# Which engine subtracts the low parts of queries and keys in an attention and mixer kernel

## The chip, the cores and the metric

The program runs on one core of a Trainium2 chip. The metric is device time in microseconds (us) of one execution, of which three were taken of the kernel before. The engines are TensorE (PE; its weight loads are PEld), VectorE (DVE), ScalarE (ACT) and GpSimd (POOL); SyncE (SP) issues most of the DMAs. Each engine works through its own instruction queue in order, and instructions on different engines are ordered by semaphores.

## The reference

Causal attention with a cumulative decay bias over 4 batches of 8 heads (576 positions, head size 64), then two feed-forward blocks. Cut to what matters here:

```
scores = scale * np.matmul(q, k.transpose(0, 1, 3, 2))
cum = np.cumsum(np.maximum(s, 0.0), axis=-1)
scores = where(causal, -1e9, scores + minimum(-(cum_i - cum_j), 0))
attn = softmax(scores)
attn_out = np.matmul(attn, v)                  # 4 x 8 heads
x = moe(x)        # mix with previous row, relu(xk @ w_k)^2 @ w_v, gate sigmoid(xr @ w_r)
out = u + relu(u @ w_ch1) @ w_ch2              # u = x + token mixing of x
```

## The kernel before

All large products are made in the fp32r format. To keep fp32 precision an operand is split: its high part is the value rounded to fp32r, its low part is the value minus the high part, also in fp32r, and a product is the sum of high*high, high*low and low*high. High parts are written by a ScalarE copy, low parts by a subtraction on VectorE or GpSimd.

The program has three stretches. First come the eight heads of batch 0 in plain fp32 (`early`, `late`). Then 24 heads of batches 1 to 3 (`visits`, with split operands) run as 108 items of one block of 128 query rows each (`attention_item`). A pair of heads shares one item for its last 64 rows each; the transposes of line 445 occur once per pair. In between stand the units of the first feed-forward block (`up`, `gate`, `down`, matrix products on line 107; `mix` on lines 509 to 512 prepares their inputs). The last stretch is the rest of the feed-forward work.

For head i, `place(i)` prepares queries and keys in two tiles. RQ holds the raw values (64 partitions, 2 x 576 columns: y = 0 queries, y = 1 keys). X1 gets the high parts on one half of its partitions (line 255, ScalarE) and the bias rows on the other. X2 gets the high part on one half (a DMA from X1, line 257, issued by SP) and the low part on the other (line 260, the subtraction). One matmul with X1 (line 300) and one with X2 (line 301) then give a block of scores. `place(i + 1)` is called with the first item of head i, thus one head ahead.

An item's chain runs over all engines. `scores`: matmuls into PSUM (3 buffers "s"), the mask and the row maximum on VectorE (line 271, which frees the buffer), then `softmax`: the exponential on ScalarE (282), a small addition on GpSimd (283), a reciprocal on VectorE (284), the scaling of P on GpSimd (285). `transposes`: P is transposed on TensorE (430, 445), its high part copied by ScalarE (439, 448, 452, 458), its low part subtracted on VectorE (440, 449, 453, 459) into PF or PT. `values`: the products with V (488) into one PSUM buffer, which ScalarE (491) and VectorE (494) empty into xt. The values V are split on VectorE (77) and GpSimd (244).

The order on each queue is not written by hand. The code gives each piece a place (`at`), and a scheduler that plays the program through against a model of the engines picks the next instruction by place and by readiness. So when one instruction goes to another engine, the order on all engines behind it can come out anew.

Of the kernel before, what the change touches and what calls it, by code (L numbers as in the profile page):

```python
# [14 lines left out]
ALU = mybir.AluOpType  # L15
# [4 lines left out]
def f32(ap):  # L20
    return ap.bitcast(F32)
# [3 lines left out]
def attention_moe_mixer(  # L25
# [16 lines left out]
    nc = tc.nc  # L42
    G, D, _, S = qk.shape
# [24 lines left out]
    def at(place):  # L68
        return tc.high_priority(tc.cur_priority - int(place * 1000))
# [62 lines left out]
    def x_tile(slot, dtype=F32):  # L132
        return qk_p.tile([128, 2 * S], dtype, tag=f"X{slot}", name=f"X{slot}").rearrange("p (t s) -> p t s", t=2)
# [79 lines left out]
    def xs(i):  # L213
        return X1[i % 2], X2[i % 2]

    def sides(i):
        a, z = slice(0, D), slice(D, 2 * D)
        return (a, z) if i % 2 == 0 else (z, a)

    def raw_qk():  # L220
        if "RQ" not in act:
            act["RQ"] = qk_p.tile([128, 8 * QC], F32, tag="HX", name="RQ")
        return act["RQ"][:, 0:2 * S].rearrange("p (t s) -> p t s", t=2)

    def load(i):
        nc.sync.dma_start(out=raw_qk()[sides(i)[0]], in_=qk[visits[i][0]])
# [19 lines left out]
    def place(i):  # L246
        g = visits[i][0]
        if i < 2:
            X2[i] = x_tile(2 + i, F32R)
        x1, x2 = xs(i)  # L250
        a, z = sides(i)
        rq = raw_qk()[a]
        nc.sync.dma_start(out=f32(x1[z][0:4]), in_=ext_d[g])
        for y in (1, 0):
            nc.scalar.activation(out=x1[a, y], in_=rq[:, y], func=AF.Copy)  # L255
            high, low = (z, a) if y else (a, z)
            nc.sync.dma_start(out=f32(x2[high, y]), in_=f32(x1[a, y]))
            for c in range(2):
                cs = slice(S * c // 2, S * (c + 1) // 2)
                nc.gpsimd.tensor_tensor(out=x2[low, y, cs], in0=rq[:, y, cs], in1=f32(x1[a, y, cs]), op=ALU.subtract)  # L260
        if i + 2 < len(visits):
            load(i + 2)

# [376 lines left out]
    def attention_item(n):  # L640
        if n < N1:
# [22 lines left out]
            if h == H - 1 and j == 2:  # L664
                with at(N0 + n):
                    place(0)
# [8 lines left out]
        if j == 0 and i + 1 < len(visits):  # L675
            with at(N0 + n):
                place(i + 1)
# [98 lines left out]
    for b in range(B):  # L776
        u = moe_units(b)
        x0 = base + PER * (b - 1) + starts[b] if b else 0
        x1 = base + PER * b + ends[b]
        if b == 0:  # L780
            x1 = base + PER + ends[0]
# [5 lines left out]
            x1 = base + 1  # L787
        else:
            x0, x1 = x0 + PER, x1 + PER
# [218 lines left out]
```

## Time and profile before

| | us |
|---|---|
| median of 3 runs | 880.22 (879.58 to 882.47) |
| the profiled execution | 883.16 |
| span of the profiled execution (first to last instruction) | 881.4 |
| TensorE busy | 850.3 (96%) |
| VectorE busy | 491.0 (56%) |
| ScalarE busy | 464.1 (53%) |
| GpSimd busy | 382.1 (43%) |

The profile is one execution. The profiled execution is 2.9 us over the median of the runs, and 1.8 us of it lie outside the span. Busy shares are means over stretches that differ: GpSimd has nothing to do after 600 us, and the subtractions that the change touches lie between 117 and 402 us. Matmuls overlap in their pipeline, so a busy TensorE is not TensorE at its peak.

### The profile page before, as it was taken

The page shows a single profiled execution, that of the slowest core. Times are in us where ns is not written, and L with a number is a line of the kernel's source. Part 1 is how long each engine was busy: PE and PEld are TensorE (multiplying, and loading weights), DVE is VectorE, ACT ScalarE, POOL GpSimd, SP SyncE. Part 2 cuts the span into 40 slices and gives each one's busy share as a digit, 9 for nine tenths or more (in the row PEclk, how much of TensorE's full clock was granted, in tenths as well). Part 3 has the DMA queues.
Part 4 walks back from the last instruction along what each step waited for, and adds up shares of the span by engine and source line. Part 5 has one row for each costly group of instructions (what it writes and reads, how often), then busy time and mean ns, then how long its engine had stood idle before and what let it go on. Part 6 is the DMA issues. An engine that isn't in the chain of part 4 may idle for free. (4 is left out here: it accounts for less than half of the span.)

```text
span 881.4 us, 17425 instructions
## 1 busy us (share of the span) xinstructions
PE 850.3 (96%) x6127; PEld 793.7 (90%) x6127; DVE 491.0 (56%) x1352; ACT 464.1 (53%) x1257; POOL 382.1 (43%) x649
## 2 busy tenths in 40 slices
PE   8889998999999999999999999899999999999998
PEld 5656766888988999989999889899999999999998
DVE  5697765477779575895559865961331222322321
ACT  4688846787785866968567873850320211211210
POOL 4565567688786766866256854630000000000000
PEclk9699999999999999999999999999999999999999
DMA  7953423134322223220144655563021112112100
GB/s 206 249 135 91 120 68 91 28 84 103 87 69 61 67 63 94 61 67 22 31 130 128 203 164 193 181 187 107 16 78 60 44 36 67 42 37 67 44 25 25
DMA packets 64982, 80.02 MB, mean 91 GB/s; under 512 B 9616, under 2 KB 51600, under 8 KB 64896
## 3 DMA queue, kind: packets, MB, share of 16 engines
q1 hardware_dynamic: 58368, 63.24, 26.1%
q0 software_dynamic: 4576, 15.08, 5.5%
q8 instruction: 48, 0.79, 0.4%
q10 hardware_dynamic: 1952, 0.60, 0.3%
q14 instruction: 38, 0.31, 0.1%
HBM read 56.50 MB, written 14.75 MB: 81 GB/s over the span
## 5 line engine op out<-in xcount | busy, mean ns | idle before, releaser
L847 ACT ACTIVATE HID<-c 128x256 fp32r<-128x256 f32 (+1 forms) x96 | 39.3, 409 | 220.4 <-PE c L107 220.3
L107 PE MATMUL vd<-KK,WV 128*128 128x256 f32 (+1 forms) x768 | 120.6, 302 | 0.0
L107 PEld LDWEIGHTS vd<-KK,WV 128*128 128x128 f32 x768 | 107.4, 191 | 4.2 <-issue 2.7
L285 POOL TENSOR_SCALAR P<-P,sum 128x128 f32<-128x128 f32 (+4 forms) x148 | 93.7, 637 | 38.4 <-DVE sum L284 29.1
L107 PE MATMUL h<-XK,WK 128*128 128x320 f32 (+1 forms) x672 | 105.7, 307 | 0.7 <-DVE XK L512 0.6
L107 PE MATMUL c<-HID,WV 128*128 128x256 f32 (+1 forms) x768 | 104.8, 291 | 0.0
L107 PE MATMUL c<-U,WK 128*128 128x256 f32 (+1 forms) x768 | 103.2, 291 | 1.4 <-DVE HID L848 1.4
L282 ACT ACTIVATE P<-P,mx 128x128 f32<-128x128 f32 (+4 forms) x148 | 86.6, 586 | 32.1 <-DVE mx L271 25.4
L107 PEld LDWEIGHTS c<-HID,WV 128*128 128x128 f32 x768 | 100.6, 188 | 0.0
L107 PEld LDWEIGHTS c<-U,WK 128*128 128x128 f32 x768 | 98.6, 188 | 1.7 <-DVE HID L848 1.7
L107 PEld LDWEIGHTS h<-XK,WK 128*128 128x128 f32 x672 | 95.3, 193 | 2.3 <-DVE XK L512 0.8
L271 DVE CUSTOM_DVE_ANT_0 P<-s,maskc 128x128 f32<-128x128 f32 (+4 forms) x148 | 72.0, 498 | 36.9 <-PE t L430 18.2
L848 DVE SCALAR_TENSOR_TENSOR HID<-c,HID 128x256 fp32r<-128x256 f32 (+1 forms) x96 | 43.8, 456 | 81.1 <-ACT HID L847 81.0
L260 POOL TENSOR_TENSOR X<-RQ,X 64x288 fp32r<-64x288 f32 x96 | 78.8, 839 | 13.1 <-ACT X L255 8.0
L912 DVE TENSOR_TENSOR ut<-c,ut 128x256 f32<-128x256 f32 (+1 forms) x32 | 14.6, 458 | 119.3 <-PE c L107 108.3
L524 POOL TENSOR_TENSOR KK<-k,KK 128x256 fp32r<-128x256 f32 (+1 forms) x64 | 54.8, 861 | 17.1 <-ACT k L523 15.5
L107 PE MATMUL r<-XR,WR 128*128 128x320 f32 (+1 forms) x384 | 61.0, 299 | 0.0
L283 POOL TENSOR_SCALAR sum<-sum 128x1 f32<-128x1 f32 (+1 forms) x148 | 33.3, 225 | 54.3 <-ACT P L282 43.0
L107 PE MATMUL c<-HID,WR 128*128 128x256 f32 (+1 forms) x384 | 54.8, 291 | 0.0
L107 PEld LDWEIGHTS r<-XR,WR 128*128 128x128 f32 x384 | 53.0, 188 | 1.2 <-issue 0.9
L107 PE MATMUL c<-U,C1A 128*128 128x256 f32 (+1 forms) x384 | 52.8, 296 | 0.1
L107 PEld LDWEIGHTS c<-U,C1A 128*128 128x128 f32 x384 | 51.5, 190 | 0.3 <-ACT U L897 0.3
(133 smaller groups left out, 1681.3 us busy)
## 6 DMA issues: line engine op xcount, KB each, us to landing
raw<-in_moe_w_ch_dram POOLq DMA_DIRECT2D x48, 256.0 KB, 3.4
RQ<-in_qk_dram SPq DMA_DIRECT2D x24, 288.0 KB
X<-X SPq DMA_DIRECT2D x48, 144.0 KB
yt<-y_d SPq DMA_DIRECT2D x16, 288.0 KB
u_d<-yt SPq DMA_DIRECT2D x16, 288.0 KB
raw<-in_moe_w_k_dram SPq DMA_DIRECT2D x8, 512.0 KB
raw<-in_moe_w_v_dram SPq DMA_DIRECT2D x16, 256.0 KB
ut<-u_d SPq DMA_DIRECT2D x32, 128.0 KB
```

Source lines behind the costliest of these rows:

```text
L107: nc.tensor.matmul(ps, a, b, start=first and i == 0, stop=last and i == n - 1)
L260: nc.gpsimd.tensor_tensor(out=x2[low, y, cs], in0=rq[:, y, cs], in1=f32(x1[a, y, cs]), op=ALU.subtract)
L271: nc.vector.tensor_tensor_reduce(out=P[0:m, c0:c1], in0=ps[0:m, 0:c1 - c0], in1=mask[0:m], scale=-scale, scalar=3.0e38 if x == 0 else mx[0 ...
L282: nc.scalar.activation(out=P[0:m, 0:w], in_=P[0:m, 0:w], func=AF.Exp, bias=mx[0:m, x:x + 1], scale=-1.0, accum_out=sm[0:m, 0:1])
L283: nc.gpsimd.tensor_scalar(out=sm[0:m, 0:1], in0=sm[0:m, 0:1], scalar1=1e-9, scalar2=1.0, op0=ALU.add, op1=ALU.mult)
L285: nc.gpsimd.tensor_scalar(out=P[0:m, 0:w], in0=P[0:m, 0:w], scalar1=sm[0:m, 1:2], scalar2=1.0, op0=ALU.mult, op1=ALU.mult)
L524: nc.gpsimd.tensor_tensor(out=kk[:, 1, m, 0:n], in0=t[:, 0:n], in1=f32(kk[:, 0, m, 0:n]), op=ALU.subtract)
L847: nc.scalar.activation(out=hi, in_=ps, func=AF.Relu)
L848: nc.vector.scalar_tensor_tensor(out=lo, in0=ps, scalar=0.0, in1=f32(hi), op0=ALU.max, op1=ALU.subtract)
L912: nc.vector.tensor_tensor(out=t, in0=ps, in1=t, op=ALU.add)
```

## The change

```diff
             high, low = (z, a) if y else (a, z)
             nc.sync.dma_start(out=f32(x2[high, y]), in_=f32(x1[a, y]))
-            for c in range(2):
-                cs = slice(S * c // 2, S * (c + 1) // 2)
-                nc.gpsimd.tensor_tensor(out=x2[low, y, cs], in0=rq[:, y, cs], in1=f32(x1[a, y, cs]), op=ALU.subtract)
+            nc.vector.tensor_tensor(out=x2[low, y], in0=rq[:, y], in1=f32(x1[a, y]), op=ALU.subtract)
```

Per head GpSimd loses four subtractions of 64 partitions by 288 columns, and VectorE gets two of 64 by 576. The numbers are the same. Lines after 260 move up by two (271 becomes 269, 300 becomes 298).

VectorE's queue where the two heads after the first batch are placed, around 144 to 152 us of the trace: the maxima (the rows ISA) of the third head's blocks stand among the two mixes. Before:

```order
L77 COPY xt<-pv 128x320
L77 CAST VV_1920<-VS 128x2x2x64
L77 CAST VV_1920<-VS 128x3x2x64
L271 ISA P_1889,mx<-s,maskc 128x128
L271 ISA mx 128x1
L509 TENSOR_SCALAR t<-xt,mu 128x320 x2
L440 TENSOR_TENSOR PF<-t,PF 128x384
L271 ISA P_1925,mx<-s,maskc 128x256
L271 ISA mx 128x1
L459 TENSOR_TENSOR PT_1791<-t,PT_1790 128x3x128
L271 ISA P_1949,mx<-s,maskc 128x384
L271 ISA mx 128x1
```

The same place now:

```order
L258 TENSOR_TENSOR X_1561<-RQ,X_1457 64x576 x2
L77 COPY xt<-pv 128x320
L77 CAST VV_1914<-VS 128x2x2x64
L438 TENSOR_TENSOR PF<-t,PF 128x384
L77 CAST VV_1914<-VS 128x3x2x64
L269 ISA P_1919,mx<-s,maskc 128x256
L269 ISA mx 128x1
L269 ISA P_1943,mx<-s,maskc 128x384
L269 ISA mx 128x1
L282 RECIPROCAL sum<-sum 128x1
L507 TENSOR_SCALAR t<-xt,mu 128x320 x2
```

Two subtractions stand ahead of the values' work, and PF and two maxima now stand ahead of the mix where they stood behind its first half.

GpSimd's queue in the same place, where P_1833 (P_1829 now) is the last block of the first pair. Before:

```order
L285 TENSOR_SCALAR P_1794<-P_1794,sum 128x512
L260 TENSOR_TENSOR X_1561<-RQ,X_1457 64x288 x4
L283 TENSOR_SCALAR sum<-sum 128x1
L244 TENSOR_TENSOR VV_1920<-VS,VV_1920 128x2x128
L244 TENSOR_TENSOR VV_1920<-VS,VV_1920 128x3x128
L283 TENSOR_SCALAR sum<-sum 128x1
L260 TENSOR_TENSOR X_1707<-RQ,X_1459 64x288 x4
L283 TENSOR_SCALAR sum<-sum 128x1
L466 MEMSET xt 128x1
L285 TENSOR_SCALAR P_1833<-P_1833,sum 128x576
```

Now:

```order
L283 TENSOR_SCALAR P_1790<-P_1790,sum 128x512
L281 TENSOR_SCALAR sum<-sum 128x1 x2
L244 TENSOR_TENSOR VV_1914<-VS,VV_1914 128x2x128
L244 TENSOR_TENSOR VV_1914<-VS,VV_1914 128x3x128
L283 TENSOR_SCALAR P_1829<-P_1829,sum 128x576
```

The scaling of that block stood behind eight subtractions and stands behind none.

VectorE's queue further on, around 198 us of the trace (P_2577 is that head's fourth block, P_2563 now). Before:

```order
L459 TENSOR_TENSOR PT_1791<-t,PT_1790 128x3x128
L512 TENSOR_TENSOR XK<-t,XK 128x256
L284 RECIPROCAL sum<-sum 128x1
L494 TENSOR_TENSOR xt<-pv,tmp 64x320
L271 ISA P_2577,mx<-s,maskc 128x512
L271 ISA mx 128x1
L459 TENSOR_TENSOR PT_1791<-t,PT_1790 128x4x128
```

Now:

```order
L457 TENSOR_TENSOR PT_1787<-t,PT_1786 128x3x128
L282 RECIPROCAL sum<-sum 128x1
L258 TENSOR_TENSOR X_1705<-RQ,X_1459 64x576
L269 ISA P_2563,mx<-s,maskc 128x512
L269 ISA mx 128x1
L258 TENSOR_TENSOR X_1705<-RQ,X_1459 64x576
L282 RECIPROCAL sum<-sum 128x1
L457 TENSOR_TENSOR PT_1787<-t,PT_1786 128x4x128
```

One subtraction now stands just ahead of a maximum, the other ahead of a reciprocal and of a low part of P.

## Rows read from the trace of the kernel before

**Rows 1.** The page, part 1: busy us (share of the span) and instructions of each engine.

```profile
PE 850.3 (96%) x6127; PEld 793.7 (90%) x6127; DVE 491.0 (56%) x1352; ACT 464.1 (53%) x1257; POOL 382.1 (43%) x649
```

**Rows 2.** Line 260: ns min/median/max; its idle time by releaser; who waited for it.

```profile
L260 POOL TENSOR_TENSOR X<-RQ,X x96: 787/805/1168, 116.9 to 402.2; 64x288 fp32r<-64x288 f32 x96
...
  ACT X L255: 8.0, 5
...
  PEld s L301: 0.6, 1
```

**Rows 3.** Windows: length, busy us (instructions) per engine, clock, DMA; two with half clock.

```profile
110.00:410.00 300.00, 287.62 (x2029) 264.01 (x2028) 214.10 (x659) 216.72 (x576) 220.96 (x387) 0.98 0.28 71
140.00:160.00 20.00, 16.45 (x82) 13.41 (x81) 9.41 (x32) 12.25 (x31) 15.78 (x25) 0.83 0.34 78
260.00:280.00 20.00, 17.56 (x128) 16.48 (x127) 18.85 (x50) 11.58 (x31) 13.41 (x27) 0.91 0.24 62
```

**Rows 4.** Waits of TensorE's weight loads, 110 to 410 us: total us, times, longest.

```profile
PEld s L300 <- DVE mx L271: 6.5, 12, 1.8
PEld pv L488 <- DVE xt L494: 2.8, 4, 1.1
PEld t L430 <- POOL P L285: 2.6, 3, 1.5
...
PEld pv L488 <- DVE PT L449: 1.9, 3, 0.8
PEld pv L488 <- DVE PF L440: 1.7, 1, 1.7
```

**Rows 5.** Windows between line 445's transposes, one a pair; columns as in rows 3.

```profile
182.50:201.40 18.90, 18.10 (x128) 16.73 (x126) 14.22 (x48) 14.24 (x37) 15.12 (x29) 1.00 0.36 93
201.40:220.20 18.80, 18.18 (x128) 16.68 (x126) 13.35 (x49) 13.96 (x36) 15.52 (x30) 1.00 0.35 91
220.20:240.80 20.60, 19.73 (x148) 18.68 (x149) 16.51 (x52) 15.73 (x43) 14.73 (x29) 1.00 0.37 93
240.80:272.20 31.40, 28.20 (x207) 26.29 (x206) 26.18 (x70) 21.93 (x62) 25.75 (x42) 0.95 0.24 60
272.20:293.00 20.80, 20.80 (x166) 20.32 (x166) 16.93 (x57) 14.82 (x39) 14.61 (x29) 1.00 0.33 86
...
346.40:371.70 25.30, 25.30 (x208) 24.58 (x206) 20.55 (x62) 24.19 (x69) 22.03 (x37) 1.00 0.30 75
371.70:398.40 26.70, 24.89 (x199) 23.97 (x197) 25.08 (x70) 15.79 (x43) 18.10 (x32) 1.00 0.24 64
```

**Rows 6.** VectorE and GpSimd groups, 110 to 410 us: busy us, mean ns | idle before.

```profile
L260 POOL TENSOR_TENSOR X<-RQ,X 64x288 fp32r<-64x288 f32 x96 | 78.8, 839 | 13.1 <-ACT X L255 8.0 <-PE s L386 2.3
...
L459 DVE TENSOR_TENSOR PT<-t,PT 128x512 fp32r<-128x512 f32 x21 | 14.3, 682 | 1.3 <-ACT PT L458 1.2
L459 DVE TENSOR_TENSOR PT<-t,PT 128x384 fp32r<-128x384 f32 x22 | 12.0, 544 | 2.1 <-ACT PT L458 2.0
L512 DVE TENSOR_TENSOR XR<-t,XR 128x320 fp32r<-128x320 f32 x12 | 8.6, 731 | 0.0
```

**Rows 7.** Timeline, one mix under GpSimd's subtractions: start us, duration us, instruction [idle before].

```profile
263.26 2.01 POOL L260 TENSOR_TENSOR X<-RQ,X 64x288 fp32r<-64x288 f32 x2
263.29 0.47 DVE L512 TENSOR_TENSOR XK<-t,XK 128x320 fp32r<-128x320 f32 x1
264.54 1.08 DVE L512 TENSOR_TENSOR XK<-t,XK 128x320 fp32r<-128x320 f32 x1
...
265.37 0.86 POOL L285 TENSOR_SCALAR P<-P,sum 128x576 f32<-128x576 f32 x1
...
266.29 0.66 PE L430 MATMUL t<-ident,P 128*128 128x128 f32 x4 [1.25 <-POOL P L285]
```

**Rows 8.** Line 510, 110 to 410 us: ns min/median/max, first and last start, forms.

```profile
L510 DVE SCALAR_TENSOR_TENSOR t<-xt,omu,t x36: 459/640/1079, 126.4 to 392.8; 128x320 f32<-128x320 f32 x20, 128x256 f32<-128x256 f32 x16
```

## The prediction

> **What bounds the kernel now.** I read the shares of the page first. TensorE is busy for 96% of the span, no other engine for more than 56% [rows 1], so in the mean TensorE is the bound, and another engine costs time only where TensorE waits for it. The subtractions in question all start between 117 and 402 us [rows 2], so I look at 110 to 410 us alone. There TensorE is busy for 287.6 of 300 us, VectorE for 214.1 and GpSimd for 221.0 [rows 3]: 12.4 us of idle TensorE are all that a better flow could win back, beside the time under half clock. The clock's mean was 0.83 in 140 to 160 us and 0.91 in 260 to 280 us [rows 3], so 20 x 0.17 = 3.4 us and 20 x 0.09 = 1.8 us of TensorE's full-speed time are missing there; both follow upon waits of TensorE.
>
> For whom does TensorE wait? The waits of its weight loads in this stretch [rows 4]: 6.5 us for the row maximum on VectorE, 2.8 us for the adding of xt, 1.9 and 1.7 us for the low parts of P, 12.9 us of VectorE together. For GpSimd it is 2.6 us (the scaled P) and 0.6 us (the subtraction itself [rows 2]), 3.2 us together. Four fifths of these waits are for the engine that is to get more work.
>
> The windows between the transposes of line 445 show the same by pair of heads [rows 5]. VectorE's share is 75%, 71% and 80% in the three pairs from 182.5 to 240.8 us, 83% in 240.8 to 272.2 us, 81% in 272.2 to 293.0 and in 346.4 to 371.7 us, and 94% in 371.7 to 398.4 us. TensorE idles for 0.8, 0.6, 0.9, 3.2, 0.0, 0.0 and 1.8 us in these seven. GpSimd is between 68% and 87% in them.
>
> **What goes.** 96 subtractions of 0.839 us, 78.8 us of GpSimd [rows 6]. GpSimd falls from 221.0 to 142 of 300 us, from 74% to 47%. Nearly nobody waited for these results as such (0.6 us, once); they cost as a queue in front of the softmax's scaling. The best place to see that is 263.26 us: two subtractions hold GpSimd for 2.01 us, the scaling of P runs behind them at 265.37 us, and the transposes at 266.29 us come after 1.25 us of idle TensorE [rows 7]. I credit the change with all of GpSimd's waits, -3.2 us.
>
> There is a second credit. Under those two subtractions one subtraction of the mix (line 512, both inputs in SBUF) took 1.08 us, while a like one that began with them took 0.47 us [rows 7]; the mean of the wide shape in the stretch is 0.731 us [rows 6]. So GpSimd's work stretches VectorE's by about 0.26 us an instruction. The stretch holds 36 calls of the mix, by its line 510 [rows 8], of three such instructions each (509, 510, 512). If all 108 are stretched alike, and line 260's share of that is its share of GpSimd's time (79/221 = 0.36), VectorE gets back 108 x 0.26 x 0.36 = 10 us.
>
> **What comes.** 48 subtractions of 64 x 576 on VectorE. The trace has none of that length. Line 459 takes 0.544 us for 384 columns and 0.682 us for 512 [rows 6], 1.08 ns a column, so 576 columns take 0.682 + 64 x 0.00108 = 0.75 us. That is the lower bound, 36 us in all. The new instruction has both inputs in SBUF, as line 512 has, so it is open to the same stretch, at GpSimd's lower share: 0.26 x 47/74 = 0.17 us, giving 0.92 us, 44 us in all. The upper bound adds the whole difference seen once, 1.08 - 0.47 = 0.61 us, to each: 1.36 us, 65 us. I take 44 us, since GpSimd's share is what the 0.731 us is a mean over. Net of the credit VectorE gets 44 - 10 = 34 us (26 to 55), and goes from 214 to 248 of 300 us, from 71% to 83%. The Trainium skill, SBUF — State Buffer, section "Who interferes with whom", has a sharper rule that speaks against this change: a VectorE instruction with two SBUF inputs and a GpSimd instruction that reads SBUF exclude each other for a whole instruction, and the later one waits. By that rule the new subtractions also hold up GpSimd's scalings of P, which the sum here leaves out; the 1.08 us of [rows 7] agrees with it in one direction, and no row here shows the other.
>
> A new wait: the subtraction waits for ScalarE's high part. GpSimd idled 8.0 us in five such waits [rows 2]. On VectorE the same wait would hold maxima and reciprocals behind it. VectorE's new queue puts the instruction where the scheduler expects the high part to be done, so I count one wait of the five, 8.0/5 = 1.6 us; the bounds are none and all 8 us. SP's load of the head after next now waits for VectorE's reading of RQ instead of GpSimd's; it is issued a head ahead, with half of a pair's 18.8 us or more [rows 5] as cover. The matmuls, their DMAs and ScalarE's work stay the same in number.
>
> **What that costs TensorE.** A pair gets four subtractions, 4 x 0.92 = 3.7 us, less about a twelfth of the 10 us (twice that in the two pairs with most of the mix, from 240.8 and from 371.7 us): +2.8 us, or +2.0 us. The shares become 17.0 of 18.9 us (90%), 16.2 of 18.8 (86%), 19.3 of 20.6 (94%), 28.2 of 31.4 (90%), 19.7 of 20.8 (95%), 23.4 of 25.3 (92%), and 27.1 of 26.7 us, over the pair's length. The trace has one pair with VectorE at 94%, where TensorE idles 1.8 of 26.7 us, 6.8% [rows 5]. I let the four pairs that reach 90% or more with little idle time now idle as much: 1.3, 1.4, 1.4 and 1.7 us instead of 0.8, 0.9, 0.0 and 0.0, +4.1 us. The pair from 240.8 us idles 3.2 us already, and I add nothing. The last must get longer to stay at 94%: 27.1/0.94 = 28.8 us, +2.1 us. By the places in the queue this is where it should show: around 198 us a subtraction now stands right ahead of a maximum, and another ahead of a low part of P, both things that TensorE waits for.
>
> **The sum.** +4.1 + 2.1 + 1.6 - 3.2 = +4.6 us on the profiled 883.16 us, 887.8 us; on the median of the runs, 2.9 us lower, 884.8 us, which is the forecast.
>
> **Rival one, faster: GpSimd was the queue that mattered.** TensorE's own waits name the last engine of a chain, and a chain goes through GpSimd twice (lines 283 and 285) but also three times through VectorE. If GpSimd at 74 to 87% made each item late, and VectorE's room in 110 to 410 us (86 us idle) takes the 34 us without new waits, the credit stands alone: -3.2 us of waits, and -1.8 us since the half clock after 266 us follows the wait for P: 875.2 us. If also the first jam goes, another -3.4 us: 871.8 us. For it: at that jam PF and two maxima now stand ahead of the mix, and the scaling of the first pair's last block no longer stands behind eight subtractions. Against it: VectorE gets four of its new subtractions in the same few microseconds, 3.7 us of work. It decides for faster if VectorE stays under some 85% in the pairs that were at 80%. The Trainium skill, GPSIMD Engine Reference, section "4.1 Engine selection", also says to put two-input elementwise work on VectorE, as GpSimd takes about twice as long; here it is 4 x 0.839 against 2 x 0.75 us a head, which agrees, but the rule counts engine time and TensorE is the bound.
>
> **Rival two, no change.** TensorE has matrix products of the feed-forward block to run in any gap, and the whole order from 117 us on comes out anew. If these products fill what VectorE leaves, gains and losses cancel: within 2.6 us of 880.2 us. For it: three of the seven pairs with much VectorE work idle under 0.7 us now [rows 5].
>
> **A worse case of the forecast.** If pairs at 90% idle as the one from 240.8 us does (3.2 of 31.4 us, 10%), the four idle 8.7 instead of 1.7 us, +7.0 us; with the last pair's 2.1 us, two waits for ScalarE, 3.2 us, and no credit, it is +12.3 us: 892.5 us.
>
> **How the numbers follow.** Forecast (VectorE becomes the bound in the dense pairs) 0.47, rival one 0.28, rival two 0.25. A difference of 0.3%, 2.6 us, is about what a measurement of this kernel can tell from no change. Each case stays on its side of that line in the main, so faster 0.29, same 0.25, slower 0.46. The forecast's own range is 882.9 to 892.5 us. The whole range goes from 874 us, inside rival one, to that 892.5 us.
>
> **What would show it.** Right: the new subtraction at 0.75 us at least and about 0.9 us in the mean; GpSimd's busy time down by 79 us, VectorE's up by some 34 us; VectorE at 90% or more in most pairs from 182 us on; TensorE's waits for the maximum, xt and the low parts of P growing from 12.9 us by 4 us or more while those for GpSimd go. Wrong: waits for VectorE that stay or fall, or a granted clock without the dips around 150 and 268 us, which would give the time to rival one; or the same idle time at other places, which is rival two. A run in which ScalarE's high part is what VectorE waits for would be slower by a step that I priced at 1.6 us only.

## The result, and the profile after

The changed kernel takes 886.76 us in the median of 6 runs (884.82 to 888.1), the kernel before 880.26 us on the same chip (6 runs). The ratio is 1.0062, with a 95% interval of 1.0041 to 1.0082: slower by 3.6 to 7.2 us (the medians lie 6.5 us apart, the ratio of all runs makes it 5.5). The profiled execution of the changed kernel took 884.82 us (span 883.0), 1.9 us under its median; that of before was 2.9 us over its own. So the two traces lie only 1.7 us apart where the kernels lie 6.5 us apart, and a time is compared between them only within a stretch.

Part 1 of the page of the changed kernel, to be held against [rows 1]:

```profile
PE 849.5 (96%) x6127; PEld 795.6 (90%) x6127; DVE 524.3 (59%) x1400; ACT 466.7 (53%) x1257; POOL 312.0 (35%) x553
```

VectorE gained 33.3 us. GpSimd lost 70.1 us, though the subtractions that left it were 78.8 us [rows 6]. The view of the new subtraction (line 258: ns min/median/max, first and last start; then the idle time ahead of it), to be held against [rows 2]:

```profile
L258 DVE TENSOR_TENSOR X<-RQ,X x48: 730/754/1054, 115.7 to 396.0; 64x576 fp32r<-64x576 f32 x48
...
  ACT X L255: 2.0, 5
```

Windows of the changed kernel with the columns of [rows 3]: the attention stretch, then the two windows in which the kernel before had TensorE's clock at half, 1.2 instead of 2.4 GHz, for a part of the time.

```profile
110.00:410.00 300.00, 288.17 (x2048) 266.19 (x2047) 239.56 (x706) 220.35 (x580) 155.53 (x292) 0.98 0.27 71
140.00:160.00 20.00, 17.11 (x89) 13.45 (x88) 14.97 (x44) 13.19 (x36) 9.08 (x19) 0.83 0.31 77
260.00:280.00 20.00, 20.00 (x164) 19.38 (x164) 17.93 (x56) 14.23 (x38) 7.99 (x19) 1.00 0.12 32
```

TensorE is busy for 288.2 us here, where it was 287.6. The waits of its weight loads in this stretch, to be held against [rows 4]:

```profile
PEld s L298 <- DVE mx L269: 6.1, 6, 1.8
...
PEld pv L486 <- DVE PT L447: 2.1, 3, 1.0
PEld h L107 <- ACT XK L509: 1.8, 2, 1.2
PEld h L107 <- DVE e L550: 1.6, 1, 1.6
PEld t L428 <- POOL sum L281: 1.5, 1, 1.5
```

The wait for the maximum did not grow (6.5 before), and those for xt and PF are no longer among the rows; waits of 1.8 and 1.6 us of the feed-forward products h, for XK and e, have come in their place. The half clock after the jam at 266 us is gone, but a like one has come between 196.6 and 218.4 us (a mean of 0.92, in the windows shown further down), and that of 140 to 160 us stays as it was (0.83): the mean of the stretch is 0.98 in both kernels. Nothing in this stretch shows a loss. By the place in the program it ends no later either: the transposes that occur once a pair (first and last start), the kernel before, then the changed one:

```profile
L445 PE MATMUL t<-ident,P x12: 270/272/273, 159.1 to 424.3; 128*64 128x128 f32 x12
L443 PE MATMUL t<-ident,P x12: 270/271/415, 151.5 to 421.3; 128*64 128x128 f32 x12
```

The 3 us ahead are not shown to be a gain: traces of kernels below that have the same order up to there put the last of these transposes at 421.3 to 424.7 us. From it to the end of the span it is 457.1 us before (881.4 - 424.3) and 461.7 us now (883.0 - 421.3). The loss lies there, behind the attention stretch, where no subtraction of queries or keys stands, and most of it in 410 to 600 us. Windows of that stretch, the kernel before:

```profile
410.00:600.00 190.00, 184.05 (x1317) 180.41 (x1317) 129.09 (x293) 120.84 (x342) 99.87 (x146) 1.00 0.47 146
```

and the changed kernel:

```profile
410.00:600.00 190.00, 180.43 (x1279) 177.55 (x1278) 134.16 (x290) 118.65 (x335) 94.72 (x143) 0.98 0.45 144
```

TensorE idles 9.6 instead of 6.0 us, and the mean clock falls from 1.00 to 0.98 (190 x 0.02 = 3.8 us of full-speed time). The two make 7.4 us, which is about the size of the result. The waits of the weight loads in 440 to 600 us of the changed kernel name them:

```profile
PEld c L107 <- DVE HID L846: 3.1, 1, 3.1
PEld t L107 <- ACT k L519: 2.5, 1, 2.5
PEld t L107 <- DVE yt L865: 2.5, 3, 1.3
```

The kernel before has none over 0.4 us there on the k that ScalarE takes out of `up` (line 521; the transposes of line 856 wait 1.0 us for the k of line 523), and 1.7 us for HID:

```profile
PEld t L107 <- DVE yt L867: 1.9, 3, 1.4
PEld c L107 <- DVE HID L848: 1.7, 1, 1.7
```

Where the wait for k comes from is to be seen on ScalarE's timeline. Line 519 (521 before) empties the accumulator of `up`, and TensorE's token-mixing product t needs that buffer. Changed kernel, ScalarE:

```profile
454.02 0.42 ACT L509 ACTIVATE XR<-t 128x256 fp32r<-128x256 f32 x1 [0.84 <-DVE t L508]
...
456.70 0.42 ACT L509 ACTIVATE XR<-t 128x256 fp32r<-128x256 f32 x1 [1.51 <-DVE t L508]
...
457.67 0.66 ACT L519 ACTIVATE k<-h 128x256 f32<-128x256 f32 x2
```

Kernel before, ScalarE:

```profile
454.95 0.42 ACT L511 ACTIVATE XR<-t 128x256 fp32r<-128x256 f32 x1 [1.13 <-DVE t L510]
...
455.94 0.73 ACT L521 ACTIVATE k<-h 128x256 f32<-128x256 f32 x2
456.57 0.41 ACT L522 ACTIVATE KK<-k 128x256 fp32r<-128x256 f32 x1
456.87 0.41 ACT L511 ACTIVATE XR<-t 128x256 fp32r<-128x256 f32 x1
```

The two emptyings stood ahead of the last copy of the mix, and stand behind it now, while that copy waits for VectorE. TensorE's timeline of the changed kernel shows this wait, and the longest one, at HID:

```profile
458.11 3.71 PE L107 MATMUL t<-YN,T 128*128 128x256 f32 x20 [2.35 <-ACT k L519]
...
567.30 6.37 PE L107 MATMUL c<-U,WK 128*128 128x384 f32 x26 [2.80 <-DVE HID L846]
```

So the theory after the traces: the move itself costs little in the attention stretch, and the scheduler's new order of the work behind it costs the time. The rival is the prediction's own: VectorE's load costs it, and the order is an accident of the trace. A third one is that fewer, longer instructions matter, whatever their engine.

### The profile page after: what moved, and what is told of

The parts are those of the page before. It is cut to its first block, busy times and chain, and to the rows that moved or that the text cites. A ratio compares the mean times of both kernels' runs of the same rounds, so it can differ in the third digit from the quotient of the medians.

```text
span 883.0 us, 17330 instructions
## 1 busy us (share of the span) xinstructions
PE 849.5 (96%) x6127; PEld 795.6 (90%) x6127; DVE 524.3 (59%) x1400; ACT 466.7 (53%) x1257; POOL 312.0 (35%) x553
## 4 chain that ended last, share of the span: by engine, by line
PE 70%; DVE 14%; issue 6%; ACT 4%; DMA 4%; POOL 2%; SPq 0%; DVEq 0%; POOLq 0%; ACTq 0%
PE c L107 33%; PE h L107 7%; PE vd L107 6%; PE t L107 3%; PE r L107 3%; PE pv L486 3%; PE t L428 2%; PE s L384 2%; DVE P L269 2%; PE pv L414 2%; DVE X L258 2%; PE s L299 2%; PE s L298 2%; DVE raw L609 2%; DMA ext_d<-e 1%
## 5 line engine op out<-in xcount | busy, mean ns | idle before, releaser
L283 POOL TENSOR_SCALAR P<-P,sum 128x128 f32<-128x128 f32 (+4 forms) x148 | 97.6, 662 | 62.4 <-DVE sum L282 54.6
L107 PEld LDWEIGHTS c<-U,WK 128*128 128x128 f32 x768 | 100.4, 190 | 3.1 <-DVE HID L846 3.1
L281 POOL TENSOR_SCALAR sum<-sum 128x1 f32<-128x1 f32 (+1 forms) x148 | 38.2, 258 | 96.7 <-ACT P L280 89.7
L298 PE MATMUL s<-X 128*128 128x128 f32 (+3 forms) x144 | 47.2, 333 | 5.0 <-DVE mx L269 5.0
## 6 DMA issues: line engine op xcount, KB each, us to landing
RQ<-in_qk_dram SPq DMA_DIRECT2D x24, 288.0 KB
yt<-y_d SPq DMA_DIRECT2D x16, 288.0 KB
u_d<-yt SPq DMA_DIRECT2D x16, 288.0 KB
```

Source lines behind the costliest of these rows:

```text
L107: nc.tensor.matmul(ps, a, b, start=first and i == 0, stop=last and i == n - 1)
L281: nc.gpsimd.tensor_scalar(out=sm[0:m, 0:1], in0=sm[0:m, 0:1], scalar1=1e-9, scalar2=1.0, op0=ALU.add, op1=ALU.mult)
L283: nc.gpsimd.tensor_scalar(out=P[0:m, 0:w], in0=P[0:m, 0:w], scalar1=sm[0:m, 1:2], scalar2=1.0, op0=ALU.mult, op1=ALU.mult)
L298: nc.tensor.matmul(ps[0:n, 0:c1 - c0], x1[:, 0, a:a + n], x1[:, 1, c0:c1], start=True, stop=False)
```

## Experiments

**How an order is kept.** In most of the kernels below the queue of every engine follows a table. An edge without a semaphore goes from each instruction to the next one of its engine in the table; only the subtractions of queries and keys are free, and the scheduler puts them where they fit. "Old order" is that of the kernel before, "new order" that of the changed kernel.

```diff
+        order = np.cumsum(steps[at:at + len(own)])
+        at += len(own)
+        for a, b in zip(order, order[1:]):
+            tc.add_manual_dep(
+                own[b], own[a].name,
+                mybir.DependencyInfo(mybir.DependencyClass.NoSync, mybir.DependencyReason.DATA),
+                reason="order",
+            )
...
         attention_moe_mixer(tc, *args)
+        keep_order(tc, nc, FREE)
```

**The engine alone, the order alone.** One kernel is the changed one with the old order as its table:

```diff
-            nc.vector.tensor_tensor(out=x2[low, y], in0=rq[:, y], in1=f32(x1[a, y]), op=ALU.subtract)
+            FREE.add(nc.vector.tensor_tensor(out=x2[low, y], in0=rq[:, y], in1=f32(x1[a, y]), op=ALU.subtract).ins.name)
...
+ORDER = (
```

> The subtractions are on VectorE as after the change, and every other instruction stands on its queue in the order of the kernel before (pinned, 48 subtractions free to stand where the scheduler puts them). Theory A, VectorE's load in the dense pairs costs the time: 885 to 888 us, about as after the change. Theory B, the load costs little and the new order of the other instructions is dear, above all between 440 and 590 us of the trace: 878 to 882 us.

The other is the kernel before with the new order as its table:

```diff
-                nc.gpsimd.tensor_tensor(out=x2[low, y, cs], in0=rq[:, y, cs], in1=f32(x1[a, y, cs]), op=ALU.subtract)
+                FREE.add(nc.gpsimd.tensor_tensor(out=x2[low, y, cs], in0=rq[:, y, cs], in1=f32(x1[a, y, cs]), op=ALU.subtract).ins.name)
...
+ORDER = (
```

> The subtractions are on GpSimd as before, and every other instruction stands in the order of the changed kernel (pinned). Theory A: 880 us or less. Theory B: 885 to 888 us, and the idle time of TensorE between 440 and 590 us as in the changed kernel.

Measured: 888.79 us (ratio 1.0096, 1.0077 to 1.0114) and 912.54 us (1.0364, 1.0347 to 1.038). Each ratio is to the kernel before on the chip of that run, where its median was 881.08 us here and 880.80 to 881.4 us below. Where nothing else is sorted anew, the move costs 7.7 us by the medians and 8.5 us by the ratio, and it shows where the prediction put it. Waits of the weight loads in 110 to 410 us of dve_in_old_order:

```profile
PEld s L298 <- DVE mx L269: 11.6, 11, 3.4
PEld pv L486 <- DVE xt L492: 2.9, 4, 1.0
...
PEld pv L486 <- DVE PF L438: 1.6, 1, 1.6
...
PEld pv L486 <- DVE PT L447: 1.4, 2, 0.8
```

The maximum is waited for 11.6 instead of 6.5 us; the four kinds make 17.5 instead of 12.9 us. In the new order GpSimd cannot do the same work in time. The same view of pool_in_new_order:

```profile
PEld t L430 <- POOL P L285: 6.0, 3, 4.6
```

So each order suits the engine that it was made for; the change cannot be priced by one of the two alone.

**The subtractions left out.** All but the first two of the 24 heads leave them out, in either order. The cut is that of the new order; in the old one the first two heads have theirs on GpSimd.

```diff
+            if i < 2:
+                FREE.add(nc.vector.tensor_tensor(out=x2[low, y], in0=rq[:, y], in1=f32(x1[a, y]), op=ALU.subtract).ins.name)
```

> Order of the kernel before (pinned); the subtractions are left out for all heads but the first two of the 24, whose low parts stay in the tiles. What they cost GpSimd in this order at most: theory A has 877 us (3.2 us of waits gone), theory B 877 to 880 us.

> Order of the changed kernel (pinned); the subtractions are left out for all heads but the first two, so neither VectorE nor GpSimd has them. Theory A: VectorE's load is gone, 876 to 880 us. Theory B: the order stays, 883 us or more.

Measured: 869.63 us (0.9881, 0.9865 to 0.9896) in the old order and 871.77 us (0.9905, 0.9882 to 0.9929) in the new one. By these floors the subtractions cost some 11 us on GpSimd in the old order (881.08 on that chip), 19.2 on VectorE in the old order, some 14 to 15 on VectorE in the new one (the changed kernel was measured beside another chip's kernel before: 15.0 by the medians, 13.8 by the ratios) and 40.8 on GpSimd in the new one. The price of GpSimd's queue, which the prediction put at 3.2 us by the waits that name GpSimd, is over three times that.

**Half the columns.** New order, VectorE, 288 of the 576 columns subtracted in all heads but the first two (the others keep what stood there):

```diff
+            w = S if i < 2 else S // 2
+            FREE.add(nc.vector.tensor_tensor(out=x2[low, y, 0:w], in0=rq[:, y, 0:w], in1=f32(x1[a, y, 0:w]), op=ALU.subtract).ins.name)
```

> Order of the changed kernel (pinned); each subtraction on VectorE covers 288 of the 576 columns for all heads but the first two, so the other low parts are stale. Without the subtractions this order took 871.8 us, with them 886.8 us. If their time on VectorE's queue is the cost, half of the 15 us goes: 879 us. If the count counts (waits for ScalarE's high part, a place in front of a maximum): 884 us or more.

Measured: 877.39 us (0.9964, 0.9946 to 0.9983). One of them takes 454 ns instead of 754 in the median; 44 of them save 44 x 0.3 = 13 us of VectorE, and some 9 us of device time (9.4 by the medians, 8.6 by the ratios). So VectorE's load is on the path in this order too, at some 0.7 us for each us of it.

**Where the order costs: before or behind the last pair.** The old order stands only behind the last transposes of the attention items (line 443), ahead of them the new order; the kernel is the changed one but for the table.

```diff
-            nc.vector.tensor_tensor(out=x2[low, y], in0=rq[:, y], in1=f32(x1[a, y]), op=ALU.subtract)
+            FREE.add(nc.vector.tensor_tensor(out=x2[low, y], in0=rq[:, y], in1=f32(x1[a, y]), op=ALU.subtract).ins.name)
...
+ORDER = (
```

> Subtractions on VectorE; all other instructions in the order of the changed kernel up to the transposes of the last pair (about 421 us), and after these in the relative order of the kernel before. If the new order of the later stretch is what costs some 5 us there: 880 to 883 us, and no more than 881 if the attention stretch really runs 2 us faster than before, as the two profiles have it. If the subtractions on VectorE are the whole of the loss: 886 to 888 us, as after the change.

Then the reverse, on the kernel before: its own order up to the last transposes (line 445), the new one behind them.

```diff
-                nc.gpsimd.tensor_tensor(out=x2[low, y, cs], in0=rq[:, y, cs], in1=f32(x1[a, y, cs]), op=ALU.subtract)
+                FREE.add(nc.gpsimd.tensor_tensor(out=x2[low, y, cs], in0=rq[:, y, cs], in1=f32(x1[a, y, cs]), op=ALU.subtract).ins.name)
...
+ORDER = (
```

> Subtractions on GpSimd; all other instructions in the order of the kernel before up to the transposes of the last pair, and after these in the relative order of the changed kernel. If the new order of the later stretch costs some 5 us: 884 to 887 us. If it costs nothing: 880 to 882 us.

Measured: 880.42 us (0.9998, 0.9978 to 1.0019) and 889.79 us (1.0084, 1.0051 to 1.0118). This settles the place. With the old order behind, the change costs nothing; with the new order behind, the kernel before loses 9 us though no subtraction has gone to another engine. The table itself is not the cause: where its order is the kernel's own, TensorE's busy time in 110 to 410 us stays as it was, 287.7 us in pool_old_then_new (287.6 before) and 288.0 in dve_new_then_old (288.2 in the changed kernel). Windows of 410 to 600 us, dve_new_then_old:

```profile
410.00:600.00 190.00, 184.52 (x1322) 181.24 (x1322) 129.95 (x293) 121.53 (x342) 99.83 (x146) 1.00 0.47 148
```

and pool_old_then_new:

```profile
410.00:600.00 190.00, 179.79 (x1264) 176.30 (x1263) 131.55 (x288) 120.03 (x340) 97.00 (x145) 0.97 0.45 139
```

Busy time and clock go with the late order and not with the engine. The latter kernel also shows the same waits as the changed one, in length and kind. Waits of the weight loads in 440 to 600 us of pool_old_then_new:

```profile
PEld c L107 <- DVE HID L848: 3.4, 2, 3.0
PEld t L107 <- DVE yt L867: 2.6, 3, 1.3
PEld t L107 <- ACT k L521: 2.5, 1, 2.5
```

**Which part of the late order.** First TensorE's late queue alone is put back to the old order in the changed kernel; the others keep the new one, and only the table says so.

```diff
-            nc.vector.tensor_tensor(out=x2[low, y], in0=rq[:, y], in1=f32(x1[a, y]), op=ALU.subtract)
+            FREE.add(nc.vector.tensor_tensor(out=x2[low, y], in0=rq[:, y], in1=f32(x1[a, y]), op=ALU.subtract).ins.name)
...
+ORDER = (
```

> The changed kernel with its own order on every engine, except that from the last pair's transposes on TensorE's queue alone takes the order of the kernel before; VectorE's and ScalarE's queues keep the changed kernel's order to the end. dve_new_then_old took the whole late order back and came out at 880.4 us, the changed kernel itself at 886.8. If what costs the 6.5 us is where TensorE's own matmuls stand, this kernel comes out near 880 to 882 us and the waits near 458 and 567 us are gone. If it is where ScalarE's and VectorE's mixing steps stand among their other work (the ScalarE copies of L519 behind those of L509 that wait for VectorE), this kernel comes out at 885 to 890 us and TensorE still shows a wait of over 2 us on ScalarE between 440 and 480 us.

Measured: 890.58 us (1.0108, 1.0088 to 1.0129), slower than either. TensorE's own old order, with the new one on the other engines, wins nothing back; the wait for ScalarE's k is still there with 1.8 us. Its 410 to 600 us:

```profile
410.00:600.00 190.00, 178.05 (x1267) 174.24 (x1266) 134.43 (x289) 118.54 (x335) 95.20 (x143) 0.99 0.46 142
```

Then only two places on ScalarE's queue are changed, those that stand in front of the two longest waits:

```
 L521 ACTIVATE k<-k 128x256
-L509 ACTIVATE XR<-t 128x256
-L75 ACTIVATE raw<-raw 128x256
-L607 ACTIVATE raw<-raw 128x256
 L519 ACTIVATE k<-h 128x256 x2
+L509 ACTIVATE XR<-t 128x256
+L75 ACTIVATE raw<-raw 128x256
+L607 ACTIVATE raw<-raw 128x256
...
 L75 ACTIVATE WR<-raw 128x256
-L75 ACTIVATE WV<-raw 128x256
 L845 ACTIVATE HID<-c_7774 128x384
+L75 ACTIVATE WV<-raw 128x256
```

> The changed kernel with its own order on every engine, except for two places on ScalarE's queue alone: near 457 us the two copies of L519 (the up products out of their accumulators) go ahead of the copy of L509 that waits for VectorE's mixing step, and near 566 us the copy of L845 (the first high part of HID) goes ahead of the rounding step of L75 that waits for VectorE's step of L609. In the changed kernel TensorE waits 2.35 us for the first and 2.80 us for the second, and its clock is halved after each. If these two places are what the late order costs, the first wait goes wholly and the second by about 1 us (VectorE's own steps stand ahead of its part of HID until 565.8 us), with what the clock gives back: 881.5 to 884.5 us. If the late order costs by its many small waits, or what is late behind these two places takes their place, as it did where TensorE's queue alone was put back (890.6 us), it stays at 885.5 to 889 us.

Measured: 885.58 us (1.0052, 1.0034 to 1.007), where the changed kernel has a ratio of 1.0062, with intervals that overlap. Waits of the weight loads in 440 to 600 us:

```profile
PEld t L107 <- DVE yt L865: 3.0, 3, 1.4
PEld c L107 <- DVE HID L846: 2.7, 1, 2.7
PEld vd L107 <- POOL KK L522: 1.5, 1, 1.5
PEld t L107 <- ACT YN L840: 1.3, 1, 1.3
```

The 2.5 us for k are gone, but 1.5 us for GpSimd's KK stand a few matmuls later, those for yt grew, and HID stays, since VectorE's own steps are ahead of it. So the places of the two longest waits do not make up the loss: a wait that is taken away here is largely replaced by the next, and only the old late order as a whole is shown to win the time back. ScalarE's or VectorE's late queue alone in old order was not tried; which of these two engines matters more stays open.

**Sharing the load.** Keys on VectorE in one operation, queries on GpSimd in two, order left to the scheduler; then the mirror of it.

```diff
+            if y:
+                nc.vector.tensor_tensor(out=x2[low, y], in0=rq[:, y], in1=f32(x1[a, y]), op=ALU.subtract)
+                continue
             for c in range(2):
```

> The low parts of the keys on VectorE (one subtraction of 64 x 576 a head), those of the queries on GpSimd (two of 64 x 288), order by the scheduler. If a subtraction costs more the fuller its engine is, the load spread over both engines is cheaper than on either: 877 to 881 us. If VectorE's load alone decides: between the two kernels, 882 to 885 us. The order comes out anew, which by the pinned kernels moves the time by 2 us by itself.

```diff
-            if y:
+            if not y:
```

> The mirror of keys_on_dve: the queries' low part on VectorE in one operation, the keys' on GpSimd in two, order left to the scheduler. keys_on_dve came out at 874.9 us. If what helps there is that each of the two engines carries half of the load, this one comes out at 873 to 878 us too. If it helps because the keys, which are subtracted first, come early from the engine with the shorter queue, this one comes out near the two unshared kernels, at 880 to 887 us.

Measured: 874.89 us (0.994, 0.992 to 0.996) and 877.89 us (0.9972, 0.9954 to 0.999). Both beat both kernels of this study. Both come out with a late order that is nearly the old one (VectorE's last 413 and 416 other instructions stand as in the kernel before, in the changed kernel only the last 162 do), and in 410 to 600 us TensorE is busy for 185.3 and 184.4 us at a clock of 1.00. Windows of keys_on_dve, the attention stretch:

```profile
110.00:410.00 300.00, 290.96 (x2084) 269.54 (x2083) 233.35 (x696) 220.96 (x589) 195.55 (x346) 0.99 0.28 71
```

TensorE is busy for 2.8 us more than in the changed kernel here. The mirror is 3 us slower than keys_on_dve, with intervals that overlap a little; why the keys would be the better half is open. In both kernels the attention stretch is sorted anew, and neither was run with a held order: how much of the gain is the sharing, and how much the order that came with it, is not shown.

**Fewer, longer operations on the old engine.** GpSimd does all, in one operation of 576 columns instead of two of 288, order left to the scheduler.

```diff
-            for c in range(2):
-                cs = slice(S * c // 2, S * (c + 1) // 2)
-                nc.gpsimd.tensor_tensor(out=x2[low, y, cs], in0=rq[:, y, cs], in1=f32(x1[a, y, cs]), op=ALU.subtract)
+            nc.gpsimd.tensor_tensor(out=x2[low, y], in0=rq[:, y], in1=f32(x1[a, y]), op=ALU.subtract)
```

> The kernel before with GpSimd's subtraction in one operation of 64 x 576 instead of two of 64 x 288, so GpSimd still does all of it, in 48 operations. The diff cuts the operations from four to two per head and moves them to VectorE at once; this kernel has only the cut. If the number of operations matters (48 issues fewer on GpSimd's queue, at some 0.05 to 0.1 us each: 2.4 to 4.8 us of its time), it comes out at 876 to 879 us. If the pieces matter the other way (another engine's GpSimd work waits behind a longer piece, 1.6 us instead of 0.8), it comes out at 882 to 886 us. If neither, within 0.3% of the kernel before, at 878 to 883 us.

Measured: 883.13 us (1.0024, 1.0007 to 1.0041), slightly slower. One piece takes 1.449 us in the mean against 2 x 0.839 = 1.68 us for two. GpSimd is busy with them for 69.6 instead of 78.8 us, and the kernel gains nothing by it, in an attention stretch that is again sorted anew. So no run shows a gain from the halved count.

## Why the prediction came out as it did

The forecast was 884.8 us, slower; 886.76 us lies inside the range and on the forecast's side, 2 us above it. The sum behind it, +4.6 us, is not how the 6.5 us came about, so that the two lie so close is luck.

**The price of the new operation** was too high: 0.92 us taken, 0.75 the lower bound, 0.754 measured in the median and 38.2 us / 48 = 0.795 in the mean of the stretch. VectorE, DVE by form, 110 to 410 us of the changed kernel:

```profile
L258 DVE TENSOR_TENSOR X<-RQ,X 64x576 fp32r<-64x576 f32 x48 | 38.2, 795 | 3.3 <-ACT X L255 2.0 <-PE s L384 0.2
...
L510 DVE TENSOR_TENSOR XR<-t,XR 128x320 fp32r<-128x320 f32 x12 | 6.6, 567 | 0.1
```

**The relief of VectorE** was about right. XR's subtraction fell from 0.731 us [rows 6] to 0.567 us, and VectorE grew by 239.6 - 214.1 = 25.5 us where 38.2 came: 12.7 us given back, for which I had 10. The net is 25.5, under the lower bound of 26 to 55 us that I gave, and not 34.

**The waits for ScalarE's high part** came to 2.0 us of VectorE's time in five waits, for which I had 1.6; of TensorE's waits only one of 0.2 us names that high part.

**What that costs TensorE** is the step that failed. I let each pair with VectorE at 90% or more idle as much as the pair that had 94%. Four of the ten windows between the transposes of line 443 from 172 us on in the changed kernel reach 90% (columns of [rows 5]); they are the second, third, fourth and fifth row here:

```profile
196.60:218.40 21.80, 19.49 (x126) 18.20 (x126) 17.30 (x54) 14.32 (x37) 10.04 (x21) 0.92 0.32 81
...
237.50:260.70 23.20, 21.90 (x173) 20.97 (x174) 21.33 (x62) 21.43 (x63) 14.64 (x26) 1.00 0.31 78
260.70:284.90 24.20, 24.20 (x200) 23.49 (x198) 22.52 (x67) 16.10 (x42) 11.29 (x23) 1.00 0.15 38
...
342.40:366.90 24.50, 24.48 (x199) 23.62 (x198) 22.23 (x64) 23.26 (x67) 14.93 (x26) 1.00 0.24 61
366.90:395.50 28.60, 27.50 (x217) 26.57 (x218) 28.13 (x80) 19.53 (x51) 14.01 (x28) 1.00 0.27 77
```

At 92%, 93%, 91% and 98% TensorE idles 1.3, 0.0, 0.0 and 1.1 us, and at 79% in the first row it idles 2.3 us. How full VectorE is in a pair does not tell what TensorE loses; how its queue is ordered does. With the order held (dve_in_old_order) the waits for VectorE grew by 17.5 - 12.9 = 4.6 us, which is within what I had worked out; the scheduler, which places the new instructions too, took that back by sorting the stretch anew (some 8 us between dve_in_old_order and dve_new_then_old).

**The credit for GpSimd** counted the waits that name GpSimd, 3.2 us. By the floor without subtractions GpSimd's work cost some 11 us: a wait names only the last engine of a chain. The trace of none_in_old_order shows a part of the rest: without the subtractions on GpSimd, TensorE's waits for the maximum, xt, PT and PF, all on VectorE, are 8.3 instead of 12.9 us, while those for GpSimd's P and X are 0.5 instead of 3.2. What came through ScalarE no run separates. Rival one said as much, and its credit was still only 3.2 us and some half clock. The other price was short by the same reasoning: 19.2 us on VectorE. The difference, 8 us, kept the forecast's sign.

**What I left out** is the stretch behind. Rival two said that the whole order comes out anew, but gave it a price of none and looked for it only in the attention stretch. By the runs the change is: the move, +7.7 us (888.79 against 881.08 on its chip); the new order of the attention stretch, -8.1 us (880.42 against 880.80, -0.4 in all); the new order behind it, +6.9 us (886.76 against 880.26, +6.5 in all). By the ratios the three are +8.5, -8.6 and +5.6 us, so each is known to some 2 us, and they hold for this sequence of steps: with the whole new order first the kernel loses 31 us, of which the move then gives back 25. The first two nearly cancel, so the result is about the size of the last one, and the prediction has no term for it. What I listed as showing me wrong, waits for VectorE that stay or fall, is what the trace shows (6.1 and 2.1 us of the four kinds, 8.2 instead of 12.9); that I would have given the time to rival one is wrong as well, since the gains there were spent elsewhere.

## What to carry to other kernels

Where a scheduler sets the order, a change of one engine's work has three prices: its own with the order held, that of the new order around it, and that of the new order far behind it; pin the queues to the old order by edges and each can be measured by itself. Price an engine's work by a run that leaves it out, not by the waits that name the engine, for these name only the last link. Where two engines are both close behind the bound, dividing a piece of work between them (874.9 us) can beat giving it to either (880.3, 886.8); here each division came with an order of its own.

## What the runs showed of the hardware

GpSimd's other work got longer when the subtractions went to VectorE. By form in 110 to 410 us, kernel before:

```profile
L283 POOL TENSOR_SCALAR sum<-sum 128x1 f32<-128x1 f32 x106 | 23.0, 217 | 33.3 <-ACT P L282 25.7 <-DVE sum L284 0.8
L285 POOL TENSOR_SCALAR P<-P,sum 128x512 f32<-128x512 f32 x24 | 17.3, 720 | 6.2 <-DVE sum L284 4.9 <-PE t L445 0.5 <-PE t L430 0.4
```

Changed kernel:

```profile
L281 POOL TENSOR_SCALAR sum<-sum 128x1 f32<-128x1 f32 x106 | 28.0, 264 | 73.9 <-ACT P L280 69.2
L283 POOL TENSOR_SCALAR P<-P,sum 128x512 f32<-128x512 f32 x24 | 18.9, 787 | 20.7 <-DVE sum L282 18.0 <-PE t L394 1.7 <-PE r L107 1.0
```

The small addition goes from 217 to 264 ns, 106 x 0.047 = 5.0 us, and the scaling of 512 columns from 720 to 787 ns. In the trace of the changed kernel 14 of the 106 additions overlap one of VectorE's new subtractions; they take 536 ns in the mean, the other 92 take 223. With the same order and the subtractions left out (none_in_new_order) the addition takes 228 and the scaling 739 ns. The rule that the prediction quotes from the Trainium skill, SBUF — State Buffer, section "Who interferes with whom", agrees with these rows in the direction that no row of before showed; that one engine's instruction keeps the other out for its whole length is not shown. With subtractions on both engines they take longer still; keys_on_dve by form:

```profile
L259 DVE TENSOR_TENSOR X<-RQ,X 64x576 fp32r<-64x576 f32 x24 | 23.6, 984 | 2.2 <-ACT X L255 1.8 <-PE s L389 0.2
L263 POOL TENSOR_TENSOR X<-RQ,X 64x288 fp32r<-64x288 f32 x48 | 43.3, 920 | 17.5 <-issue 12.2 <-PE s L389 2.4 <-POOL P L288 1.3
```

VectorE's operation takes 0.984 us instead of 0.795, GpSimd's 0.920 instead of 0.839, and this is the fastest of the kernels that do all of the work.

The granted clock does not follow the length of a single wait. In the changed kernel it is 0.96 in 440 to 480 and in 560 to 600 us, each with one long wait of TensorE (2.35 and 2.80 us); in two_places a wait of 2.40 us at 569 us stands in a window at 1.00, while 480 to 520 and 520 to 560 us, whose longest wait is 1.12 us, are at 0.96. Their drops follow two shorter waits each, 1.04 and 1.12 us at 492 to 496 us, 1.03 and 0.65 us at 517 to 519 us.
